# A hand-ordered attention and feed-forward kernel: GpSimd's queue, its loads, the sketches and the task list rearranged

## The chip, the cores and the metric

The kernel runs on one core of a Trainium2 chip. The metric is device time in microseconds for one execution, lower is better. Several executions were timed, and one execution was recorded by the hardware profiler; the profile's times count from the start of its span.

## The reference

Polynomial-sketch attention, then a feed-forward layer with SiLU. There are 4 batches, 4 heads, a sequence of 1088 and a head size of 32; the sketches S1 and S2 are 8 by 32. The feed-forward part has 4352 tokens of width 128 and an inner width of 2048.

```python
def phi(x):
    a = np.einsum('rd,bhsd->bhsr', S1, x)
    b = np.einsum('rd,bhsd->bhsr', S2, x)
    return np.einsum('bhsi,bhsj->bhsij', a, b).reshape(*x.shape[:-1], r * r)
q_p, k_p = phi(q), phi(k)
kv = np.einsum('bhsf,bhsd->bhfd', k_p, v)
z = np.sum(k_p, axis=2)
num = np.einsum('bhsf,bhfd->bhsd', q_p, kv)
den = np.einsum('bhsf,bhf->bhs', q_p, z)[..., None] + 1e-06
attn = num / den                                   # [B, H, S, D]
x = attn.transpose(0, 2, 1, 3).reshape(B * S, H * D)
h = x @ w_in
out = (h * (1.0 / (1.0 + np.exp(-h)))) @ w_out     # float32 [4352, 128]
```

## The kernel before

The order of all work is written out by hand. `ORDER` is a list of tasks, read from top to bottom; each task emits its instructions, and every engine executes what it was given in that order. An engine stops at an instruction whose inputs are not there, and all that stands behind it on that engine waits too. Loads are emitted ahead of the whole list: on SyncE's queue (SP) K of batch 0 in two pieces, the first part of Q, V, the four quarters of w_in, the rest of Q, then K and Q of batches 1 to 3; on ScalarE's queue the two sketches; on GpSimd's queue w_out and V of batches 1 to 3, which these loads convert from float32 to bf16. GpSimd's queue first has its memsets and masks, then these loads, and after them whatever tasks give it.

Some loads are held. `begin(..., after)` adds a dependency on another load's landing: w_out waits for the second quarter of w_in, V of batch b waits for Q of batch b−1, K of batch b for the same, and Q of batch b for K of batch b.

The tasks, with the engine that does most of them; the first number is the batch, and a pair p0 p1 is a range of rows of 64 tokens:

- `weights` (DVE) transposes the sketches into ST and masks them into WK, the weights of pk and of the constant columns of WQ; `weights2` (DVE) makes the mask hm4 and L4 (S2 repeated for four heads and masked); `wq_const` (GpSimd) copies WK into the constant columns of WQ for all four batches, eight small copies.
- `kt` (DVE) transposes K; `pk` (PE) multiplies by WK; `tk` (DVE) transposes the result back to SBUF; `kp` (DVE) forms the products of features, four pieces a batch.
- `zs` (PE) sums for z, `zc` copies it out of PSUM (A is ScalarE, V is VectorE), `mm` (PE) multiplies by L4, and `mk` (DVE) writes the last columns of WQ. `kv` (PE) accumulates kv; `kw` (DVE) or `kw_act` (ScalarE) copies it out with masks.
- `qt` (DVE) transposes Q; `pq` (PE) multiplies by WQ; `tq` (DVE) transposes back; `dn` (DVE, four instructions) forms and applies the denominator; `qo` (DVE) forms the feature products; `pt` (DVE) transposes them; `nm` (PE) multiplies by kv; `xc` copies the result to xT, the tokens of the feed-forward part.
- `wic` (ScalarE) converts a quarter of w_in to bf16, `vc0` half of V of batch 0.
- `f1 c s` (PE), `sl c s` (ScalarE, SiLU) and `f2 c s` (PE) are the feed-forward part for chunk c of tokens and slice s of the inner width; `ot` (DVE) transposes the output of a chunk and stores it through SP's queue. There are ten chunks; the first three have 256, 384 and 448 tokens.
- `zeros n` (PE) are n matmuls of zeros, 128 by 128 by 128, whose result nobody reads.

A tile named with H takes one of the two PSUM buffers of f1. The pool of f1 has two buffers, those of f2's output, of pk, pq and nm (psP), and of z, m and kv (psA) one each.

Of the kernel before, what the change touches and what calls it, by code (L numbers as in the profile page):

```python
# [28 lines left out]
f2 0 1, f2 0 2, qo 0 10 17, f1 1 0, sl 1 0, f1 1 4
zs 1, f1 1 2, sl 1 4, f2 0 3, f1 1 1, zc 1 A  # L30
pk 2, sl 1 2, ot 0, pt 0 10 17, sl 1 1, f1 1 6
qt 1 0 34, f2 1 0, f1 1 3, tk 2, mm 1, f2 1 1
sl 1 6, f1 1 5, f2 1 2, mk 1, kp 1 0 1, nm 0 10 17
sl 1 3, pq 1 0 8 H, kp 1 1 1, sl 1 5, xc 0 10 17 A, tq 1 0 8
kp 1 0 0, f1 1 7, kp 1 1 0, f2 1 3, pq 1 8 17, f1 2 0
dn 1 0 8, f2 1 4, sl 1 7, f1 2 4, sl 2 0, kv 1
f1 2 1, sl 2 4, f2 1 5, f1 2 7, sl 2 1, f2 1 6
f2 1 7, kw 1, qo 1 0 8, f1 2 6, sl 2 7, ot 1
pt 1 0 8, zs 2, f1 2 3, sl 2 6, zc 2 V, tq 1 8 17
f2 2 0, f1 2 2, sl 2 3, dn 1 8 17, mm 2, nm 1 0 8  # L40
xc 1 0 8 V, f1 2 5, mk 2, f2 2 1, sl 2 2, kt 3 0 34
sl 2 5, qt 2 0 34, f2 2 2, f2 2 3, f1 3 1, qo 1 8 17
f2 2 4, f1 3 0, f2 2 5, sl 3 1, f2 2 6, f1 3 6
f2 2 7, sl 3 0, ot 2, pt 1 8 17, sl 3 6, f1 3 2
pq 2 0 8, f1 3 5, f2 3 0, sl 3 2, tq 2 0 8, f1 3 3
sl 3 5, kp 2 0 0, f2 3 1, nm 1 8 17, f1 3 7, sl 3 3
f2 3 2, sl 3 7, xc 1 8 17 V, f1 3 4, pk 3, dn 2 0 8
kp 2 1 1, f1 4 1, f2 3 3, sl 3 4, f1 4 3, kp 2 1 0
kp 2 0 1, f2 3 4, sl 4 1, sl 4 3, f2 3 5, f1 4 4
f2 3 6, f1 4 0, kv 2, qo 2 0 8, sl 4 4, tk 3  # L50
pt 2 0 8, kw 2, f1 4 2, f2 3 7, sl 4 0, pq 2 8 17 H
sl 4 2, ot 3, tq 2 8 17, nm 2 0 8, f1 4 6, f2 4 0
xc 2 0 8 V, f1 4 5, zs 3, sl 4 6, sl 4 5, f1 5 2
f2 4 1, zc 3 V, sl 5 2, f1 5 4, dn 2 8 17, qo 2 8 17
qt 3 0 34, f2 4 2, pt 2 8 17, f2 4 3, kp 3 0 1, f1 4 7
kp 3 1 0, mm 3, sl 5 4, f1 5 0, sl 4 7, f2 4 4
sl 5 0, f2 4 5, f1 5 3, f2 4 6, f1 5 1, mk 3
f2 4 7, sl 5 3, ot 4, sl 5 1, f1 5 6, nm 2 8 17
xc 2 8 17 V, sl 5 6, f1 5 5, f2 5 0, sl 5 5, f2 5 1
f1 5 7, f2 5 2, f1 6 0, pq 3 0 8, sl 5 7, kp 3 1 1  # L60
f1 6 3, f2 5 3, f2 5 4, sl 6 0, f1 6 2, sl 6 3
f2 5 5, tq 3 0 8, kp 3 0 0, sl 6 2, dn 3 0 8, f1 6 4
qo 3 0 8, f2 5 6, f1 6 1, pt 3 0 8, kv 3, sl 6 4
f1 6 6, sl 6 1, f2 5 7, sl 6 6, kw 3, ot 5
f1 6 7, pq 3 8 17, nm 3 0 8 H, sl 6 7, f2 6 0, f1 6 5
f2 6 1, xc 3 0 8 V, sl 6 5, f1 7 3, sl 7 3, f2 6 2
f2 6 3, f1 7 2, tq 3 8 17, f2 6 4, f1 7 0, dn 3 8 17
sl 7 2, sl 7 0, qo 3 8 17, pt 3 8 17, f2 6 5, f2 6 6
f1 7 1, f2 6 7, ot 6, f1 7 4, sl 7 1, sl 7 4
nm 3 8 17, f1 7 7, f2 7 0, sl 7 7, f1 7 5, sl 7 5  # L70
xc 3 8 17 V, f2 7 1, f1 8 0, sl 8 0, f2 7 2, f1 7 6
f2 7 3, f1 8 1, f2 7 4, sl 7 6, f1 8 2, sl 8 1
f2 7 5, f1 8 7, f2 7 6, f2 7 7, sl 8 2, f1 8 3
sl 8 7, ot 7, sl 8 3, f1 8 4, f2 8 0, sl 8 4
f2 8 1, f1 8 5, f2 8 2, sl 8 5, f1 8 6, f2 8 3
f2 8 4, f1 9 0, sl 8 6, f2 8 5, f1 9 1, sl 9 0
f2 8 6, f2 8 7, sl 9 1, f1 9 2, f1 9 3, sl 9 2
# [12 lines left out]
def kernel(  # L90
# [65 lines left out]
    def begin(eng, dst, src, after=None):  # L156
        ins = eng.dma_start(dst, src)  # L157
# [10 lines left out]
    def load_v(eng, b, dst, after=None):  # L168
        for c in range(4):
            n = min(NC, NY - c * NC)  # L170
            ins = begin(eng, dst[32 * c: 32 * (c + 1), :, :n, :].rearrange("p h n d -> p h (n d)"),
                        AP(tensor=v.tensor, offset=v[b, 0, c * NC].offset,
                           ap=[[NY * D, 32], [S * D, H], [1, n * D]]), after)
        return ins

    def sketch(eng, i, src):
        return eng.dma_start(T12[:, i, :], AP(tensor=src.tensor, offset=src.offset,
                                              ap=[[0, P // R], [D, R], [1, D]]))
# [12 lines left out]

# [22 lines left out]
    prev = q0b
    for b in range(1, B):
        load_v(nc.gpsimd, b, Vb[b], prev)
        kb = load_kq(nc.sync, b, k, Kx, after=prev)
        prev = load_kq(nc.sync, b, q, Qx, after=kb)  # L220

    nc.scalar.activation(out=warm, in_=warm, func=ACT.Silu)


# [11 lines left out]
            nc.tensor.matmul(t["zps"][:, :ncol], zw, zw[:, :ncol], start=True, stop=True)  # L236

    def weights():
        vcopy_in = T12.rearrange("p a d -> p (a d)")
        nc.vector.transpose(out=ST.rearrange("p a c i -> p (a c i)"), in_=vcopy_in)  # L240
        nc.vector.tensor_tensor(out=WK, in0=ST[:, :, 0:2, :].rearrange("p a h i -> p h a i"),
                                in1=bcast(bcast(hm2, 2, 2), 3, R), op=ALU.mult)

    def weights2():
        nc.vector.tensor_reduce(out=hm4, in_=E8.rearrange("p s h -> p h s"), axis=AX.X, op=ALU.add)  # L245
        nc.vector.tensor_tensor(out=L4, in0=bcast(T12[:, 1, :], 1, H), in1=bcast(hm4, 2, D),
                                op=ALU.mult)

    def wq_const():
        for b in range(B):  # L250
            nc.gpsimd.tensor_copy(out=WQ[b][:, :, 0:R].rearrange("p h (i e) -> p h e i", e=2),
                                  in_=WK[:, :, 0, :].rearrange("p h (e i) -> p h e i", e=2))
            nc.gpsimd.tensor_copy(out=WQ[b][:, :, R: 2 * R], in_=WK[:, :, 1, :])  # L253

# [21 lines left out]
        nc.vector.transpose(out=t["pk", b].rearrange("p n r h a i -> p r n (h a i)"),  # L278
                            in_=t["pk_ps", b][:, :, :NC * 32].rearrange("p r (n f) -> p r n f", f=32))

    def kp(b, e, h):
        s = t["pk", b][:, :, :, h].rearrange("p n r a i -> p (n r) a i")
        o = t["kp", b][:, :, :, e, h].rearrange("p n r j i -> p (n r) j i")
        nc.vector.tensor_tensor(out=o, in0=bcast(s[:, :, 0, 4 * e: 4 * e + 4], 2, R),  # L284
                                in1=bcast(s[:, :, 1], 3, 4), op=ALU.mult)
# [86 lines left out]

    def qo(b, p0, p1):
        fa, fb, fw = feats(b, p0, p1)
        if p0 == 0:
# [2 lines left out]
        nc.vector.tensor_tensor(out=t["qp", b][:, p0:p1].rearrange("p y r j i -> p (y r) j i"),  # L378
                                in0=bcast(fa, 2, R), in1=bcast(fb, 3, R), op=ALU.mult)
# [127 lines left out]
```

## Time and profile before

| what | value |
|---|---|
| median of 3 runs | 122.09 us (121.97 to 122.43) |
| profiled execution | 121.77 us, its span 119.1 us |
| busy in the span | PE 88.3, ACT 73.3, DVE 67.6, GpSimd 12.1 us |
| mean granted TensorE clock | 0.912 |
| moved by DMA | 8.81 MB read from HBM, 2.23 MB written |

Busy time is the sum of the spans of an engine's instructions; instructions that issue a DMA are not counted as busy on the queues of SP and ScalarE. Lines L157, L230 and L227 are those of helpers (all loads, and the copies on ScalarE and VectorE), so there one goes by the tile. In the waits, a line names the engine that stood still, the one that released it, and the total time, the number of times, and the longest. The chain is followed back from the last instruction to what released each step.

### The profile page before, as it was taken

The numbers are of one execution on the slowest core, as the hardware profiler recorded it, in microseconds if no ns is written. First come the engines' busy times: TensorE is split into PE (matmuls) and PEld (weight loads), VectorE is DVE, ScalarE is ACT, GpSimd is POOL, SyncE is SP. The second block draws the span as 40 slices with busy tenths as digits, with TensorE's granted clock in tenths as the row PEclk, the third lists the DMA queues.
The fourth block names the chain that finished last, engine by engine and source line by source line (L and its number), as shares of the span: only waits on it lengthen the run. The fifth ranks groups of instructions, "written<-read, shape, count | busy, mean of one in ns | idle before, by whom it ended". The sixth has DMA issues, their size and how long they took to land.

```text
span 119.1 us, 2189 instructions
## 1 busy us (share of the span) xinstructions
PE 88.3 (74%) x857; PEld 48.1 (40%) x864; DVE 67.6 (57%) x128; ACT 73.3 (62%) x91; POOL 12.1 (10%) x47
## 2 busy tenths in 40 slices
...
GB/s 99 288 265 279 125 277 122 151 243 195 148 192 129 6 0 0 44 6 3 66 6 19 61 0 0 90 3 0 88 0 6 47 41 70 18 1 67 21 102 22
DMA packets 24857, 9.81 MB, mean 82 GB/s; under 512 B 21392, under 2 KB 23184, under 8 KB 24848
## 3 DMA queue, kind: packets, MB, share of 16 engines
...
q10 hardware_dynamic: 288, 0.03, 0.2%
q14 instruction: 3, 0.02, 0.1%
HBM read 8.81 MB, written 2.23 MB: 93 GB/s over the span
## 4 chain that ended last, share of the span: by engine, by line
PE 42%; DMA 23%; DVE 17%; ACT 8%; issue 2%; SPq 2%; POOL 2%; POOLq 0%; ACTq 0%; DVEq 0%
PE o_ps L437 18%; PE h_ps L419 16%; DMA Qx<-in_q_dram 11%; DMA Kx<-in_k_dram 9%; ACT g L426 8%; DVE qp L378 3%; DMA T<-in_S_dram 3%; DVE kp L284 2%; DVE PQ L358 2%; PE zps L236 2%; DVE KT L258 2%; SPq L157 2%; POOL Vb L157 2%; PE pq_ps L352 2%; DVE qT L384 1%
## 5 line engine op out<-in xcount | busy, mean ns | idle before, releaser
L426 ACT ACTIVATE g<-h_ps 128x1024 bf16<-128x1024 f32 (+2 forms) x72 | 65.5, 981 | 7.8 <-PE h_ps L419 5.7
L419 PE MATMUL h_ps<-xT,w_in_bf 128*128 128x512 bf16 (+4 forms) x156 | 39.8, 347 | 0.5
L437 PE MATMUL o_ps<-g,w_out_bf 128*128 128x512 bf16 (+4 forms) x157 | 37.5, 346 | 0.4
L437 PEld LDWEIGHTS <-w_out_bf 128*128 128x128 bf16 x160 | 15.2, 98 | 14.5 <-issue 0.7
L419 PEld LDWEIGHTS <-w_in_bf 128*128 128x128 bf16 x160 | 14.2, 98 | 15.2 <-issue 5.6
L352 PE MATMUL pq_ps<-QT,WQ 64*64 64x288 f32 (+3 forms) x48 | 4.0, 409 | 21.6 <-POOL WQ L253 21.6
L358 DVE STREAM_TRANSPOSE PQ<-pq_ps 128x576 f32<-128x576 f32 (+3 forms) x6 | 4.0, 669 | 23.0 <-PE pq_ps L352 23.0
L335 ACT ACTIVATE KVw<-kv_ps,hm 64x64 bf16<-64x64 f32 (+1 forms) x6 | 1.5, 306 | 22.8 <-PE kv_ps L316 22.7
L443 DVE STREAM_TRANSPOSE o_tt<-o_ps 128x512 f32<-128x512 f32 (+4 forms) x10 | 6.3, 635 | 13.9 <-PE o_ps L437 13.8
L236 PE MATMUL zps<-zw 128*128 128x128 bf16 x112 | 10.7, 264 | 1.1 <-POOL hm L196 1.1
L284 DVE TENSOR_TENSOR kp<-pk 128x576 bf16<-128x576 f32 x16 | 11.3, 740 | 0.0
L352 PEld LDWEIGHTS pq_ps<-QT,WQ 64*64 64x64 f32 x48 | 1.4, 143 | 23.4 <-POOL WQ L253 21.7
L236 PEld LDWEIGHTS <-zw 128*128 128x128 bf16 x112 | 9.0, 123 | 3.7 <-issue 2.5
L378 DVE TENSOR_TENSOR qp<-PQ 128x1024 bf16<-128x1024 f32 (+4 forms) x9 | 10.3, 1146 | 0.1
L157 POOL DMA_DIRECT2D Vb<-in_v_dram x12 | 6.5, 546 | 15.2 <-DMA Qx<-in_q_dram 15.2
L384 DVE STREAM_TRANSPOSE qT<-qp 128x512 f32<-128x512 f32 (+4 forms) x9 | 5.9, 659 | 0.1
L258 DVE STREAM_TRANSPOSE KT<-Kx 128x1088 f32<-128x1088 f32 (+2 forms) x5 | 5.3, 1063 | 0.0
L341 DVE STREAM_TRANSPOSE QT<-Qx 128x1088 f32<-128x1088 f32 (+2 forms) x5 | 5.3, 1057 | 0.0
L230 ACT ACTIVATE Vb<-Vx 128x576 bf16<-128x576 f32 x2 | 1.3, 675 | 5.0 <-DMA Vx<-in_v_dram 5.0
L227 DVE CAST xT<-num_ps 128x576 bf16<-128x576 f32 (+1 forms) x5 | 3.6, 714 | 0.2
L271 PE MATMUL h_ps<-KT,WK 64*32 64x288 f32 x16 | 2.4, 682 | 1.8 <-DVE hm L245 1.8
L316 PEld LDWEIGHTS <-kp 128*128 128x128 bf16 x72 | 3.1, 107 | 0.7 <-DVE kp L284 0.2
...
## 6 DMA issues: line engine op xcount, KB each, us to landing
Kx<-in_k_dram SPq DMA_DIRECT2D x3, 544.0 KB, 3.6
Qx<-in_q_dram SPq DMA_DIRECT2D x3, 544.0 KB, 4.1
...
Vb<-in_v_dram POOLq DMA_DIRECT2D x9, 72.0 KB, 3.8
w_out_bf<-in_moe_w_out_dram POOLq DMA_DIRECT2D x1, 512.0 KB, 7.0
...
```

Source lines behind the costliest of these rows:

```text
L157: ins = eng.dma_start(dst, src)
L236: nc.tensor.matmul(t["zps"][:, :ncol], zw, zw[:, :ncol], start=True, stop=True)
L258: nc.vector.transpose(out=KT[b % 2][:, y0 * 32: y1 * 32], in_=Kx[b][:, y0:y1, :].rearrange("p a d -> p (a d)"))
L284: nc.vector.tensor_tensor(out=o, in0=bcast(s[:, :, 0, 4 * e: 4 * e + 4], 2, R), in1=bcast(s[:, :, 1], 3, 4), op=ALU.mult)
L352: nc.tensor.matmul(t["pq_ps", b, p0][64 * g: 64 * (g + 1), r, :cols].rearrange("p (y x) -> p y x", x=32), w[rs, :], qv[rs, g, p0:p1, :], s ...
L358: nc.vector.transpose(out=PQ[b % 2][:, p0:p1].rearrange("p y r f -> p r y f"), in_=t["pq_ps", b, p0][:, :, :cols].rearrange("p r (y f) -> ...
L378: nc.vector.tensor_tensor(out=t["qp", b][:, p0:p1].rearrange("p y r j i -> p (y r) j i"), in0=bcast(fa, 2, R), in1=bcast(fb, 3, R), op=ALU ...
L384: nc.vector.transpose(out=dst.rearrange("p r (y x) -> p y r x", x=32), in_=src)
L419: nc.tensor.matmul(h[:, i, :], w_in_bf[:, j * P: (j + 1) * P], xT[:, t0: t0 + ntok], start=True, stop=True)
L426: nc.scalar.activation(out=gv, in_=t.pop(("h", c, s)), func=ACT.Silu)
L437: nc.tensor.matmul(op[c][:, :ntok], w_out_bf[:, j, :], g[:, i, :], start=(j == 0), stop=(j == NJ - 1))
L443: nc.vector.transpose(out=o_tt[:, :ntok], in_=op[c][:, :ntok])
```

## The change

GpSimd's copies of constants (`wq_const`) stay a task, and the GpSimd loads become tasks too: `wo` (w_out) and `lv b` (V of batch b) now come behind `wq_const` in the list. None of the loads is held, except w_out, which waits for V of batch 0. K and Q of batches 1 to 3 are issued by SP in one go after the others.

w_out is read in groups of four rows: partition p of group i holds rows 512 i + 4 p to 512 i + 4 p + 3. So that f1 makes the inner columns in the same arrangement, `wic` reads every fourth column of its quarter of w_in.

The sketches are loaded to 32 partitions, S1 twice and S2 twice, and four transposes spread them over the 128 partitions; a third load puts S2 on all partitions, for L4, whose product moves from VectorE to GpSimd.

The task list is new throughout; its start is shown. The counts of zero matmuls are different at each place.

```diff
 ORDER = """
-weights, kt 0 0 18, zeros 28, pk 0 0 2 H, weights2, kt 0 18 34
-vc0 2 4, qt 0 0 8, vc0 0 2, zeros 6, pk 0 2 4, tk 0
-kp 0 1 1, zeros 13, zs 0, kp 0 0 0, zc 0 A, kp 0 0 1
-wic 1, wq_const, wic 0, zeros 10, mm 0, mk 0
-wic 2, zeros 6, pq 0 0 4, kp 0 1 0, zeros 4, kv 0
-tq 0 0 4, dn 0 0 4, wic 3, qt 0 8 34, zeros 22, pq 0 4 10 H
-qo 0 0 4, pt 0 0 4, pq 0 10 17, kw_act 0, zeros 3, nm 0 0 4 H
-xc 0 0 4 A, tq 0 4 10, zeros 10, f1 0 0, sl 0 0, f1 0 1
-kt 1 0 34, dn 0 4 10, zeros 10, f1 0 3, sl 0 1, sl 0 3
-tq 0 10 17, f2 0 0, qo 0 4 10, f1 0 2, pt 0 4 10, sl 0 2
-pk 1, dn 0 10 17, nm 0 4 10 H, tk 1, xc 0 4 10 A, kt 2 0 34
+weights, vc0 0 2, kt 0 0 18, kt 0 18 34, zeros 33, pk 0 0 2 H
+weights2, zeros 3, pk 0 2 4, qt 0 0 8, tk 0, zeros 13
+zs 0, vc0 2 4, kp 0 0 0, wic 1, wic 0, zc 0 V
+wq_const, kp 0 0 1, zeros 5, mm 0, kp 0 1 0, mk 0
+zeros 14, pq 0 0 4 H, kp 0 1 1, tq 0 0 4, zeros 7, kv 0
+dn 0 0 4, kw_act 0, qo 0 0 4, wic 3, pt 0 0 4, wic 2
+zeros 27, nm 0 0 4 H, qt 0 8 34, xc 0 0 4 V, zeros 7, pq 0 4 10
+f1 0 0, tq 0 4 10, sl 0 0, f1 0 1, wo, sl 0 1
+pq 0 10 17, dn 0 4 10, qo 0 4 10, tq 0 10 17, zeros 3, f1 0 2
+f2 0 0, f1 0 3, sl 0 2, f2 0 1, pt 0 4 10, kt 1 0 34
+sl 0 3, nm 0 4 10 H, f2 0 2, xc 0 4 10 A, f2 0 3, dn 0 10 17
+f1 1 0, sl 1 0, ot 0, f1 1 3, sl 1 3, pk 1
+qo 0 10 17, f1 1 1, tk 1, f1 1 6, kt 2 0 34, f2 1 0
+sl 1 1, qt 1 0 34, lv 1, lv 2, f1 1 7, f2 1 1
...
-    T12 = const.tile([P, 2, D], FP32, name="T12")
-    ST = const.tile([P, 2, 4, R], FP32, name="ST")
+    T16 = const.tile([32, D], FP32, name="T16")
+    T2 = const.tile([P, D], FP32, name="T2")
+    ST = const.tile([P, 2, 2, R], FP32, name="ST")
...
-    def sketch(eng, i, src):
-        return eng.dma_start(T12[:, i, :], AP(tensor=src.tensor, offset=src.offset,
-                                              ap=[[0, P // R], [D, R], [1, D]]))
+    def sketch(eng, dst, src, count):
+        return eng.dma_start(dst, AP(tensor=src.tensor, offset=src.offset,
+                                     ap=[[0, count], [D, R], [1, D]]))
...
-    sketch(nc.scalar, 0, S1)
-    sketch(nc.scalar, 1, S2)
+    sketch(nc.scalar, T16[0:16, :], S1, 2)
+    sketch(nc.scalar, T16[16:32, :], S2, 2)
     load_kq(nc.sync, 0, k, Kx, 18, NY)
     load_kq(nc.sync, 0, q, Qx, 0, 8)
-    load_v(nc.sync, 0, Vx)
-    wi = []
+    sketch(nc.scalar, T2, S2, P // R)
+    v0 = load_v(nc.sync, 0, Vx)
     for i in range(4):
-        wi.append(begin(nc.sync, w_in_f[:, i * CH:(i + 1) * CH], moe_w_in[:, i * CH:(i + 1) * CH]))
-    q0b = load_kq(nc.sync, 0, q, Qx, 8, NY)
+        begin(nc.sync, w_in_f[:, i * CH:(i + 1) * CH], moe_w_in[:, i * CH:(i + 1) * CH])
+    load_kq(nc.sync, 0, q, Qx, 8, NY)
+    for b in range(1, B):
+        load_kq(nc.sync, b, k, Kx)
+        load_kq(nc.sync, b, q, Qx)
...
-    wo = begin(nc.gpsimd, w_out_bf, moe_w_out.rearrange("(j p) m -> p j m", p=P), wi[1])
-    prev = q0b
-    for b in range(1, B):
-        load_v(nc.gpsimd, b, Vb[b], prev)
-        kb = load_kq(nc.sync, b, k, Kx, after=prev)
-        prev = load_kq(nc.sync, b, q, Qx, after=kb)
-
...
     def weights():
-        vcopy_in = T12.rearrange("p a d -> p (a d)")
-        nc.vector.transpose(out=ST.rearrange("p a c i -> p (a c i)"), in_=vcopy_in)
-        nc.vector.tensor_tensor(out=WK, in0=ST[:, :, 0:2, :].rearrange("p a h i -> p h a i"),
+        for i in range(4):
+            nc.vector.transpose(out=ST[32 * i: 32 * (i + 1)].rearrange("p a h i -> p (a h i)"), in_=T16)
+        nc.vector.tensor_tensor(out=WK, in0=ST.rearrange("p a h i -> p h a i"),
                                 in1=bcast(bcast(hm2, 2, 2), 3, R), op=ALU.mult)
 
     def weights2():
         nc.vector.tensor_reduce(out=hm4, in_=E8.rearrange("p s h -> p h s"), axis=AX.X, op=ALU.add)
-        nc.vector.tensor_tensor(out=L4, in0=bcast(T12[:, 1, :], 1, H), in1=bcast(hm4, 2, D),
-                                op=ALU.mult)
+        nc.gpsimd.tensor_tensor(out=L4, in0=bcast(T2, 1, H), in1=bcast(hm4, 2, D), op=ALU.mult)
...
+    def wo():
+        begin(nc.gpsimd, w_out_bf.rearrange("p (i e) m -> p i (e m)", e=4),
+              moe_w_out.rearrange("(i p e) m -> p i (e m)", p=P, e=4), v0)
+
+    def lv(b):
+        load_v(nc.gpsimd, b, Vb[b])
...
-    def wic(i, n=4):
-        w = DFF // n
-        acopy(w_in_bf[:, i * w: (i + 1) * w], w_in_f[:, i * w: (i + 1) * w])
+    def wic(i):
+        cols = slice(i * CH, (i + 1) * CH)
+        acopy(w_in_bf[:, cols].rearrange("p (e m) -> p e m", e=4),
+              w_in_f[:, cols].rearrange("p (m e) -> p e m", e=4))
```

Further down the new list, `lv 3` and the rest of the tasks follow in an order of their own; xc 1 0 8 and zc 2 are on ScalarE there instead of VectorE. That `qo` makes its tiles where they aren't there yet, and that `kp` can take another engine, changes no instruction.

More of the change, by code (lines that the diff above doesn't have):

```diff
@@ L27 @@
-tq 0 10 17, f2 0 0, qo 0 4 10, f1 0 2, pt 0 4 10, sl 0 2
-pk 1, dn 0 10 17, nm 0 4 10 H, tk 1, xc 0 4 10 A, kt 2 0 34
[L29 to L77, printed above, removed]
@@ L78 @@
-ot 8, f2 9 0, f2 9 1, sl 9 3, f2 9 2, f2 9 3
-ot 9
+weights, vc0 0 2, kt 0 0 18, kt 0 18 34, zeros 33, pk 0 0 2 H
[7 more added lines that the diff above has]
+pq 0 10 17, dn 0 4 10, qo 0 4 10, tq 0 10 17, zeros 3, f1 0 2
@@ new lines @@
+f2 0 0, f1 0 3, sl 0 2, f2 0 1, pt 0 4 10, kt 1 0 34
[3 more added lines that the diff above has]
+sl 1 1, qt 1 0 34, lv 1, lv 2, f1 1 7, f2 1 1
+sl 1 6, pt 0 10 17, f1 1 2, sl 1 7, sl 1 2, zs 1
+pk 2, f1 1 5, zc 1 A, mm 1, tk 2, f1 1 4
+sl 1 5, sl 1 4, f2 1 2, f2 1 3, nm 0 10 17 H, xc 0 10 17 A
+mk 1, zs 2, kp 1 1 0, pq 1 0 8, kp 1 0 0, f1 2 3
+f1 2 1, kp 1 0 1, f2 1 4, zc 2 A, f2 1 5, f2 1 6
@@ new lines @@
+sl 2 3, sl 2 1, f1 2 0, f2 1 7, sl 2 0, f1 2 5
+tq 1 0 8, kp 1 1 1, sl 2 5, kv 1, f1 2 2, sl 2 2
+dn 1 0 8, ot 1, f2 2 0, f1 2 4, sl 2 4, qo 1 0 8
+kw 1, f2 2 1, f1 2 6, sl 2 6, f2 2 2, pt 1 0 8
+kt 3 0 34, pq 1 8 17, nm 1 0 8 H, f1 2 7, f2 2 3, xc 1 0 8 A
+sl 2 7, f2 2 4, f1 3 0, sl 3 0, tq 1 8 17, pk 3
+f1 3 1, f2 2 5, lv 3, sl 3 1, dn 1 8 17, qo 1 8 17
+pt 1 8 17, f1 3 5, mm 2, f2 2 6, tk 3, f1 3 7
+mk 2, sl 3 5, sl 3 7, f2 2 7, f1 3 2, ot 2
+nm 1 8 17, f1 3 3, f2 3 0, sl 3 2, f2 3 1, qt 2 0 34
@@ new lines @@
+sl 3 3, xc 1 8 17 V, f1 3 6, kp 2 1 1, f2 3 2, sl 3 6
+f1 4 2, kp 2 0 0, pq 2 0 8, f1 4 3, tq 2 0 8, kp 2 1 0
+sl 4 2, f2 3 3, sl 4 3, f1 3 4, pq 2 8 17, kp 2 0 1
+sl 3 4, f1 4 7, sl 4 7, dn 2 0 8, kv 2, tq 2 8 17
+f1 4 1, sl 4 1, f2 3 4, qo 2 0 8, kw 2, f1 4 0
+f2 3 5, sl 4 0, f2 3 6, pt 2 0 8, f2 3 7, ot 3
+f1 4 6, f1 4 4, nm 2 0 8, zs 3, f2 4 0, sl 4 6
+sl 4 4, xc 2 0 8 V, dn 2 8 17, qt 3 0 34, f1 4 5, f2 4 1
+f1 5 1, f2 4 2, qo 2 8 17, sl 4 5, zc 3 V, sl 5 1
+f2 4 3, f1 5 0, sl 5 0, f2 4 4, kp 3 1 1, f1 5 5
@@ new lines @@
+f2 4 5, f2 4 6, f1 5 4, sl 5 5, sl 5 4, f2 4 7
+pt 2 8 17, f1 5 7, mm 3, nm 2 8 17, kp 3 1 0, f1 5 3
+sl 5 7, ot 4, mk 3, f2 5 0, f1 5 2, xc 2 8 17 V
+sl 5 3, sl 5 2, pq 3 0 8, f1 5 6, sl 5 6, f2 5 1
+tq 3 0 8, f1 6 1, sl 6 1, pq 3 8 17, f1 6 4, kp 3 0 0
+f2 5 2, dn 3 0 8, sl 6 4, f1 6 2, f2 5 3, tq 3 8 17
+qo 3 0 8, kp 3 0 1, f2 5 4, f1 6 0, sl 6 2, f2 5 5
+f1 6 7, pt 3 0 8, kv 3, dn 3 8 17, sl 6 0, kw 3
+sl 6 7, f1 6 5, f2 5 6, f2 5 7, f1 6 6, sl 6 5
+nm 3 0 8, f1 6 3, ot 5, xc 3 0 8 V, sl 6 6, f2 6 0
```

24 lines of the change are left out of this document (18 added, 6 removed).

## The prediction

> **What bounds the kernel now.** I read the busy time by stages first, then the waits, then GpSimd's own timeline, then the chain that ended last. The stages (window, its length, then busy time of PE, PEld, DVE, ACT and POOL, granted clock, DMA share, GB/s):
>
> ```profile
> 0.00:12.20 12.20, 8.84 (x117) 6.25 (x117) 5.42 (x13) 4.37 (x8) 4.50 (x27) 1.00 0.75 228
> 12.20:33.30 21.10, 0.02 (x3) 0.02 (x3) 0.62 (x1) 0.62 (x2) 6.87 (x15) 0.60 0.85 185
> ...
> 39.20:58.00 18.80, 18.26 (x252) 10.94 (x250) 18.26 (x38) 16.18 (x22) 0.00 (x0) 1.00 0.06 12
> 58.00:87.70 29.70, 29.42 (x236) 13.14 (x241) 26.66 (x48) 26.40 (x28) 0.00 (x0) 1.00 0.19 32
> 87.70:113.90 26.20, 25.89 (x168) 12.89 (x168) 11.67 (x21) 23.78 (x26) 0.00 (x0) 1.00 0.20 35
> ```
>
> From 12.2 to 33.3 us nothing computes: PE 0.02, DVE 0.62, ACT 0.62 of 21.1 us. After 39.2 PE is busy 73.6 of 74.7 us, so that part can hardly shrink. The waits (engine, line, releaser; total, times, longest) say what ends the hole:
>
> ```profile
> DVE PQ L358 <- PE pq_ps L352: 23.0, 2, 21.2
> ...
> PE pq_ps L352 <- POOL WQ L253: 21.6, 1, 21.6
> POOL Vb L157 <- DMA Qx<-in_q_dram: 15.2, 3, 7.9
> ```
>
> The first pq matmul waits 21.6 us for WQ, eight small GpSimd copies. GpSimd's timeline (start, length) shows why they are late, and SyncE's pieces of the chain show what GpSimd's loads wait for:
>
> ```profile
> 9.91 1.29 POOL L157 DMA_DIRECT2D w_out_bf<-in_moe_w_out_dram  x1 [5.56 <-DMA w_in_f<-in_moe_w_in_dram]
> ...
> 30.71 2.15 POOL L157 DMA_DIRECT2D Vb<-in_v_dram  x4 [5.90 <-DMA Qx<-in_q_dram]
> 32.90 0.20 POOL L251 COPY WQ<-WK 128x16 f32<-128x16 f32 x1
> ```
> ```profile
> 6.20 6.08 DMA Qx<-in_q_dram
> ...
> 12.30 6.78 DMA Kx<-in_k_dram
> ```
>
> The copies stand behind the V loads on GpSimd, and each V load is held until the Q load of the batch before has landed. Their input WK has been there since 5.3 us.
>
> **The change part by part.** *(a) The constant copies go ahead of the loads.* To place the new start I follow the path to the first f1 with durations of these rows:
>
> ```profile
> 0.82 1.27 ACTq L177 DMA_DIRECT2D T<-in_S_dram  x2
> ...
> 1.08 3.17 PE L236 MATMUL zps<-zw 128*128 128x128 bf16 x28 [1.08 <-POOL hm L196]
> ...
> 4.75 0.25 DVE L240 STREAM_TRANSPOSE ST<-T 128x64 f32<-128x64 f32 x1 [4.75 <-DMA T<-in_S_dram]
> ...
> 5.21 0.77 DVE L258 STREAM_TRANSPOSE KT<-Kx 128x576 f32<-128x576 f32 x1
> ...
> 6.04 1.18 PE L271 MATMUL h_ps<-KT,WK 64*32 64x288 f32 x8 [1.79 <-DVE hm L245]
> ...
> 6.27 0.70 DVE L258 STREAM_TRANSPOSE KT<-Kx 128x512 f32<-128x512 f32 x1
> ...
> 8.61 1.26 ACT L230 ACTIVATE Vb<-Vx 128x576 bf16<-128x576 f32 x2 [4.99 <-DMA Vx<-in_v_dram]
> ...
> 9.15 0.78 DVE L278 STREAM_TRANSPOSE pk<-h_ps 128x576 f32<-128x576 f32 x1 [1.86 <-PE h_ps L271]
> ...
> 9.97 2.10 DVE L284 TENSOR_TENSOR kp<-pk 128x576 bf16<-128x576 f32 x3
> ...
> 10.65 2.17 ACT L230 ACTIVATE w_in_bf<-w_in_f 128x512 bf16<-128x512 f32 x4
> ...
> 11.98 0.17 DVE L306 TENSOR_TENSOR WQ<-m_ps,hm 128x16 f32<-128x16 f32 x1
> ```
>
> The eight copies end about 1.2 us after they start (32.90 to 34.06). In the new order GpSimd first does L4 (a 128x128 product, moved from DVE). Its bounds: 0.2 us, one of the copies, up to 1.6 us, if it cost eight times a copy of 16 columns. Both inputs are there by some 6.5 us (the reduce follows both KT transposes; T2 is a third issue behind the two that took 1.27). So WQ's constants are ready by 7.9 to 9.3 us; mk, the last writer of WQ, comes later, and the copies cost nothing. If they slipped past 11.4 us, every further us would count in full.
>
> *(b) Sketches in 32 rows.* The two issues end at 2.1 (0.82 + 1.27) and the second lands 2.65 us later, at 4.75. The small T16 pair lands between 3.4 (half of that way) and 4.75 us (as now); I take 4.2. Four small transposes replace one of 0.25: between 0.25 and 1.0 us together, I take 0.6, between the ends because a fixed part is repeated. With 0.2 for WK, KT starts at 5.0 instead of 5.21 (bounds 3.9 to 6.0): worth little. The reduce and L4 no longer stand between the KT halves, which end at 6.4 instead of 6.97.
>
> *(c) Zero matmuls.* In the old list 28+6+13+10+6+4+22+3+10+10 = 112, in the new one 33+3+13+5+14+7+27+7+3 = 112, and still 128 columns each: only their places change. The first 28 took 0.113 us each, so 33 end at 4.8, before pk is ready at 5.8. The two pk halves (1.18 each, three zeros between) end at 8.4 at the old pace, or at 6.9 if the longer run has brought the matmuls up to the pace of later ones; I take 8.1, nearer the old pace, since a gap of 1 us follows as before. tk starts at 8.1 instead of 9.15.
>
> *(d) The new order from there*, on DVE: tk 0.78 to 8.9; three kp of 0.70, the z copy and mk of 0.17 each: mk ends at 11.35. So pq 0 0 4 starts at about 11.4 instead of 33.28. The next rows give the rest:
>
> ```profile
> 33.28 0.70 PE L352 MATMUL pq_ps<-QT,WQ 64*64 64x128 f32 x8 [21.57 <-POOL WQ L253]
> ...
> 34.05 0.45 DVE L358 STREAM_TRANSPOSE PQ<-pq_ps 128x256 f32<-128x256 f32 x1 [21.24 <-PE pq_ps L352]
> ...
> 34.32 1.17 PE L316 MATMUL kv_ps<-Vb,kp 128*128 128x64 bf16 x18
> ...
> 35.51 1.04 DVE L341 STREAM_TRANSPOSE QT<-Qx 128x832 f32<-128x832 f32 x1
> 35.53 1.59 ACT L335 ACTIVATE KVw<-kv_ps,hm 128x64 bf16<-128x64 f32 x6 [22.70 <-PE kv_ps L316]
> 36.47 0.65 DVE L378 TENSOR_TENSOR qp<-PQ 128x512 bf16<-128x512 f32 x1
> 37.16 0.45 DVE L384 STREAM_TRANSPOSE qT<-qp 128x256 f32<-128x256 f32 x1
> ...
> 38.43 0.31 PE L393 MATMUL h_ps<-qT,KVw 64*64 64x128 bf16 x8
> ...
> 38.79 0.39 ACT L230 ACTIVATE xT<-h_ps 128x256 bf16<-128x256 f32 x1 [1.67 <-PE h_ps L393]
> ...
> 39.23 1.04 PE L419 MATMUL h_ps<-xT,w_in_bf 128*128 128x256 bf16 x8
> ```
>
> DVE: kp 0.70 to 12.05, tq 0.45, dn 1.0 (34.50 to 35.51), qo 0.65, pt 0.45: 14.6. PE and ACT: seven zeros and kv, then kw_act 1.59, end at about 15.0; nm ends at 15.4. DVE does qt 0 8 34 (1.04) first, 15.65, then xc 0 0 4, which moves from ACT to DVE: 16.1. This qt needs the second Q0 load, landed at 12.28 now; w_out, now released by V0 (8.61) and not by w_in (9.91), runs beside it. It may land up to 3 us later with w_out wholly ahead of it; 14.6 is when it is wanted. I add 0.3. **First f1 at 16.4 instead of 39.23.**
>
> *(e) The rest.* From the first f1 to the end it is 79.9 us now (119.1 − 39.2), with PE busy for all but 1.1 us of it up to 113.9. The tasks are the same. tq 0 4 10 and most of a kt move behind the first f1, and tq 1 8 17 and dn 1 8 17 move behind xc 1 0 8: DVE's work up to xc 1 0 8 stays within 0.4 us, set off by seven fewer zeros after the first f1. So 79.9 again.
>
> *(f) Loads without holds, w_out in groups of four rows.* What is late next is data. The sizes (KB each, median us to landing) and the rates:
>
> ```profile
> Kx<-in_k_dram SPq DMA_DIRECT2D x3, 544.0 KB, 3.6
> ...
> Vb<-in_v_dram POOLq DMA_DIRECT2D x9, 72.0 KB, 3.8
> w_out_bf<-in_moe_w_out_dram POOLq DMA_DIRECT2D x1, 512.0 KB, 7.0
> ```
> ```profile
> 9.00:12.00 3.00, 2.71 (x71) 2.38 (x67) 2.81 (x5) 2.29 (x6) 1.29 (x1) 1.00 0.72 272
> 12.00:15.00 3.00, 0.00 (x0) 0.00 (x0) 0.82 (x3) 0.82 (x2) 2.16 (x4) 1.00 1.33 130
> 15.00:18.00 3.00, 0.00 (x0) 0.00 (x0) 0.00 (x0) 0.00 (x0) 0.00 (x0) 0.70 1.33 281
> ```
>
> DVE wants K1 at about 20 us (after xc: tq, dn, qo, tq, pt), K2 some 4.5 us later, at 24.3 (kt 1, dn, qo, tk). After Q0 at 12.3 three loads of 544 KB are in front of K2's end, and at worst all of w_out and V (512 + 12 x 72 KB): 3.08 MB. At 272 GB/s K2 lands at 23.6, no stall. At 130 GB/s for GpSimd's 1.41 MB (the window when w_out in its old form ran almost alone) it is 5.6 us later, a stall of 4.9. The window with K1 and V1 together shows 281, and w_out's pieces become longer, so I stay near the first end: 0.3 us. In groups of four rows wic reads every fourth column; no row shows such a read. Bounds: the 0.62 a copy of the contiguous form, or twice that. wic 3 and wic 2 follow kw_act at 15.0 and end at 16.1, the first Silu comes at 17.0, so up to 0.9 us more is hidden.
>
> A rule beside that last row: the Trainium skill, Advanced Engine Details and Errata, section Memory Cachelines, says SBUF wants at least two hits on a 16-byte line for full speed, and this read makes one. No run here shows such a read yet. If each copy doubled, the first Silu would come 0.2 us later and the sum would be 99.8.
>
> **Sum:** 16.4 + 79.9 + 0.3 = 96.6 us of span. The profiled execution took 121.77 for a span of 119.1, 2.67 around it: 99.3. The median of the runs (122.09) is 0.3 above the profiled one: **99.6 us**, faster by 22.5.
>
> **The rivals.**
> *Loads in each other's way* (0.20). Without holds V2 and V3 run beside K1, Q1, K2 though they are wanted much later. For it: K1 took 6.78 us beside w_out and V1, where a K load's median is 3.6. If each of K1, Q1, K2 took 6.8 from 12.3 on, K2 would land at 32.6 were they in series; at 130 GB/s for GpSimd's bytes at 29.2. DVE then waits 4.9 us at kt 2, PE runs out of work of the first two chunks, and the time is 102 to 106, centre 104.
> The Trainium skill, DMA: Bandwidth & Descriptors, section Queues, rings and completion order, says each DMA engine goes round its queues packet by packet; K1's 6.78 agrees, and by that rule this rival holds while GpSimd's queue is full.
> *A quicker start* (0.08): T16 at 3.4, pk at the later pace, f1 at 14.5 and PE's 1.1 idle us gone: 96 or less.
> *The change doesn't do what it says* (0.04): the copies run early, but another wait, on L4, T2 or V0, holds POOL or PE; a landing of 7 us as for w_out would cost 7 to 15 us of the gain: 107 to 115.
> *Slower* (0.03): the hole goes, but the granted clock stays low. In the hole it was 0.60 on average; with other gaps between the zeros it could fail to rise. PE's 73.6 us at clock c take 73.6/c; the gain of 22.5 is gone when c is below 73.6/96.1 = 0.77. At 0.6 the end would be 49 us later, 149. Against it: 1.00 in all windows once PE is fed.
>
> **How the numbers follow.** Forecast 0.65, rivals 0.20, 0.08, 0.04, 0.03. The forecast's own range is 97.0 to 101.5 (f1 between 15 and 18). With most of the load rival: 96.0 to 104.0. Half a per cent, 0.6 us, is about what can be told from no change. Faster 0.95, same 0.02, slower 0.03: only the clock rival, and the tail of the last but one, are not faster.
>
> **What would show it.** (a) GpSimd's copies before 10 us, PE's wait for them gone from the waits. (b) DVE's first transpose at 4.2 or sooner; four of them under 0.25 each. (c) the pk groups 1.18 or shorter. (d) pq at 11.4, first f1 at 16.4. (e) PE busy over 98% from there to 5.2 us before the end. (f) no idle DVE in front of kt 1, kt 2, qt 1 with a K or Q load as releaser; ACT's wic copies 0.62. It is wrong if PE or DVE idles between 16 and 35 us for a load, if Q0's second part lands after 15, or if the granted clock after 15 us is under 1.00.

## The result and the profile after

The changed kernel took 104.77 us (103.92 to 105.12, four runs) against 122.03 for the kernel before: a ratio of 0.858, interval 0.851 to 0.865. It is faster by 17 us where 22.5 were forecast, and it lies outside the range of 96 to 104. The profiled execution took 105.12 us with a span of 103.1. Single executions of some kernels ran over 1.5% above the fastest of the same kernel; the times and ratios here and below leave them out.

The stages, with the same columns as those of before:

```profile
0.00:12.20 12.20, 8.09 (x107) 5.63 (x107) 4.56 (x13) 4.89 (x6) 7.21 (x40) 0.86 0.75 218
12.20:18.30 6.10, 5.39 (x100) 4.46 (x101) 5.55 (x13) 3.17 (x8) 2.15 (x5) 1.00 1.06 354
18.30:23.20 4.90, 2.28 (x27) 1.36 (x23) 4.63 (x9) 3.36 (x4) 0.00 (x0) 1.00 1.10 338
23.20:28.00 4.80, 4.77 (x32) 2.93 (x32) 1.90 (x7) 1.68 (x3) 1.81 (x4) 0.64 1.05 165
28.00:58.00 30.00, 29.78 (x332) 14.13 (x330) 28.88 (x51) 26.70 (x34) 0.90 (x2) 1.00 0.18 27
58.00:97.90 39.90, 39.24 (x282) 18.59 (x274) 22.20 (x41) 35.96 (x39) 0.00 (x0) 1.00 0.22 38
```

The hole of 21 us is gone. A small one has come: from 18.3 to 23.2 us PE is busy for 2.28 of 4.9 us, and in the 4.8 us after it the granted clock is 0.64 and DVE and ACT are busy for 1.90 and 1.68 us only. The waits name it, and the issues give the landing (KB, us):

```profile
POOL Vb L158 <- DMA w_out_bf<-in_moe_w_out_dram: 9.1, 1, 9.1
...
PE o_ps L439 <- DMA w_out_bf<-in_moe_w_out_dram: 2.6, 1, 2.6
```
```profile
Kx<-in_k_dram SPq DMA_DIRECT2D x3, 544.0 KB, 10.4
Qx<-in_q_dram SPq DMA_DIRECT2D x3, 544.0 KB, 14.8
...
w_out_bf<-in_moe_w_out_dram POOLq DMA_DIRECT2D x1, 512.0 KB, 13.5
```

In the timeline the load goes out at 9.64 and the first f2 starts 13.6 us later:

```profile
8.20 0.40 POOL L242 TENSOR_TENSOR L<-T,hm 128x128 f32<-128x128 f32 x1 [3.84 <-DVE hm L241]
...
9.64 0.94 POOL L158 DMA_DIRECT2D w_out_bf<-in_moe_w_out_dram  x1
...
13.54 0.45 PE L354 MATMUL h_ps<-QT,WQ 64*64 64x128 f32 x8 [0.26 <-DVE WQ L308]
...
16.66 2.14 ACT L226 ACTIVATE w_in_bf<-w_in_f 128x512 bf16<-128x512 f32 x2
...
18.26 1.05 PE L421 MATMUL h_ps<-xT,w_in_bf 128*128 128x256 bf16 x8
...
23.23 0.61 PE L439 MATMUL o_ps<-g,w_out_bf 128*128 128x256 bf16 x4 [2.65 <-DMA w_out_bf<-in_moe_w_out_dram]
```

pq starts at 13.54 and waits no longer for GpSimd's copies; the first f1 starts at 18.26. From there to the end it is 84.8 us, where the kernel before took 79.9.

### The profile page after: what moved, and what is told of

Read it like the earlier page. It is cut to its first block, busy times and chain, and to the rows that moved or that the text cites. A ratio compares the mean times of both kernels' runs of the same rounds, so it can differ in the third digit from the quotient of the medians.

```text
span 103.1 us, 2192 instructions
## 1 busy us (share of the span) xinstructions
PE 89.6 (87%) x864; PEld 47.1 (46%) x864; DVE 67.7 (66%) x130; ACT 75.8 (73%) x91; POOL 12.1 (12%) x48
## 4 chain that ended last, share of the span: by engine, by line
PE 63%; DMA 16%; DVE 9%; ACT 1%; POOL 1%; ACTq 1%; issue 1%; DVEq 0%; POOLq 0%
PE o_ps L439 28%; PE h_ps L421 25%; DMA w_out_bf<-in_moe_w_out_dram 13%; DMA T<-in_S_dram 3%; PE pq_ps L354 3%; PE num_ps L395 2%; ACT g L428 1%; DVE PQ L360 1%; DVE kp L286 1%; PE z_ps L295 1%; PE pk_ps L273 1%; DVE KT L260 1%; ACTq L178 1%; DVE o_tt L445 1%; DVE qp L380 1%; PE kv_ps L318 1%
## 5 line engine op out<-in xcount | busy, mean ns | idle before, releaser
L439 PE MATMUL o_ps<-g,w_out_bf 128*128 128x512 bf16 (+4 forms) x160 | 38.7, 355 | 2.8 <-DMA w_out_bf<-in_moe_w_out_dram 2.6
L421 PE MATMUL h_ps<-xT,w_in_bf 128*128 128x512 bf16 (+4 forms) x160 | 40.8, 351 | 0.1
L232 PE MATMUL zps<-zw 128*128 128x128 bf16 x112 | 9.6, 249 | 1.1 <-POOL hm L199 1.1
L232 PEld LDWEIGHTS <-zw 128*128 128x128 bf16 x112 | 8.1, 115 | 3.5 <-issue 2.3
L360 DVE STREAM_TRANSPOSE PQ<-pq_ps 128x512 f32<-128x512 f32 (+3 forms) x8 | 5.7, 714 | 1.7 <-PE pq_ps L354 1.6
L354 PE MATMUL pq_ps<-QT,WQ 64*64 64x256 f32 (+3 forms) x64 | 5.3, 401 | 0.1
L236 DVE STREAM_TRANSPOSE ST<-T 32x32 f32<-32x32 f32 x4 | 0.8, 202 | 5.6 <-DMA T<-in_S_dram 5.6
L226 ACT ACTIVATE w_in_bf<-w_in_f 128x512 bf16<-128x512 f32 x4 | 4.3, 1122 | 0.1
## 6 DMA issues: line engine op xcount, KB each, us to landing
w_out_bf<-in_moe_w_out_dram POOLq DMA_DIRECT2D x1, 512.0 KB, 13.5
```

Source lines behind the costliest of these rows:

```text
L354: nc.tensor.matmul(t["pq_ps", b, p0][64 * g: 64 * (g + 1), r, :cols].rearrange("p (y x) -> p y x", x=32), w[rs, :], qv[rs, g, p0:p1, :], s ...
L360: nc.vector.transpose(out=PQ[b % 2][:, p0:p1].rearrange("p y r f -> p r y f"), in_=t["pq_ps", b, p0][:, :, :cols].rearrange("p r (y f) -> ...
L421: nc.tensor.matmul(h[:, i, :], w_in_bf[:, j * P: (j + 1) * P], xT[:, t0: t0 + ntok], start=True, stop=True)
L439: nc.tensor.matmul(op[c][:, :ntok], w_out_bf[:, j, :], g[:, i, :], start=(j == 0), stop=(j == NJ - 1))
```

## The experiments

**Why does w_out land 13.5 us after its issue, when it took 7.0 before?** The theory: with the holds gone, six K and Q loads of 544 KB stand in SP's queue, and w_out shares the DMA engines with them. Three kernels tell it from its rivals.

K and Q of batches 1 to 3 held until w_out has landed (`kq_held`):

```diff
     def wo():
-        begin(nc.gpsimd, w_out_bf..., moe_w_out..., v0)
+        wo_in = begin(nc.gpsimd, w_out_bf..., moe_w_out..., v0)
+        for b in range(1, B):          # and no longer ahead of the tasks
+            load_kq(nc.sync, b, k, Kx, after=wo_in if b == 1 else None)
+            load_kq(nc.sync, b, q, Qx)
```

> The changed kernel with K and Q of batches 1 to 3 issued only after w_out has landed; all else as changed. Theory (w_out's landing, 13.5 us after its issue, is late because it takes turns on the DMA engines with the six K and Q loads that stand in SP's queue): w_out lands 6 to 8 us after its issue, near 16.5 us, PE's wait of 2.65 us for it and the half clock behind it go, time 100 to 101.5. Rival one (V1 and V2, issued right behind w_out on its own queue, slow it): landing still 12 us or more, time 104 to 107. Rival two (the form with groups of four rows is slow by itself): the same as rival one. If K1 then comes too late (wanted at 22 us), DVE stalls in front of kt 1 and the time stays near 104 though w_out landed early.

Measured: 100.32 us, a ratio to before of 0.826 (0.818 to 0.835), span 98.4. w_out's issue and landing, and the stretch behind the first f1:

```profile
DMA to landing us min/median/max: 8.2/8.2/8.2
```
```profile
18.20:23.20 5.00, 4.74 (x55) 3.41 (x52) 4.70 (x10) 4.74 (x6) 2.55 (x5) 1.00 0.98 305
23.20:28.00 4.80, 4.60 (x87) 2.23 (x84) 4.70 (x10) 4.17 (x6) 0.00 (x0) 1.00 1.11 350
```

The landing is back at 8.2 us, though w_out still comes in groups of four rows and the V loads still stand behind it on its queue. PE is busy for 4.74 of 5.0 us where it was 2.28 of 4.9, and the clock stays at 1.00. The span is 4.7 us shorter. First f1 is at 18.19, as in the changed kernel, and the rest takes 80.2 us.

V of batches 1 to 3 held for w_out instead (`v_held`):

```diff
     def wo():
-        begin(nc.gpsimd, w_out_bf..., moe_w_out..., v0)
+        t['wo'] = begin(nc.gpsimd, w_out_bf..., moe_w_out..., v0)
     def lv(b):
-        load_v(nc.gpsimd, b, Vb[b])
+        load_v(nc.gpsimd, b, Vb[b], t['wo'])
```

> The changed kernel with V of batches 1 to 3 issued only after w_out has landed; K and Q free as changed. Theory (turns with SP's K and Q loads): w_out still lands 12 us or more after its issue, time 104 to 106. Rival one (its own queue's V loads): landing 6 to 9 us after the issue, time 100 to 102.

Measured: 105.27 us (ratio 0.865, 0.861 to 0.869). w_out lands 15.3 us after its issue, and PE waits 4.4 us:

```profile
PE o_ps L439 <- DMA w_out_bf<-in_moe_w_out_dram: 4.4, 1, 4.4
```

That is no earlier than in the changed kernel: the V loads behind w_out on its own queue aren't the cause.

w_out in single rows as before, w_in copied in plain order (`wo_rows`):

```diff
-        begin(nc.gpsimd, w_out_bf.rearrange("p (i e) m -> p i (e m)", e=4),
-              moe_w_out.rearrange("(i p e) m -> p i (e m)", p=P, e=4), v0)
+        begin(nc.gpsimd, w_out_bf, moe_w_out.rearrange("(j p) m -> p j m", p=P), v0)
-        acopy(w_in_bf[:, cols].rearrange("p (e m) -> p e m", e=4),
-              w_in_f[:, cols].rearrange("p (m e) -> p e m", e=4))
+        acopy(w_in_bf[:, cols], w_in_f[:, cols])
```

> The changed kernel with w_out read in single rows as before and w_in converted in its plain order (no strided read). Theory (turns with other queues): with four times as many and shorter pieces w_out gets a smaller share of each turn and lands later, 16 us or more after its issue, and the time is 106 to 110, though the four copies of w_in take 0.62 us again instead of 1.12. Rival two (the grouped form is slow): w_out lands 7 to 9 us after its issue as in the kernel before, time 100 to 102. Rival three (the strided read of w_in is what costs): time 1 to 2 us lower whatever w_out does.

Measured: 107.80 us (ratio 0.884, 0.879 to 0.889). Landing 16.5 us after the issue, PE's wait 5.7. So the single rows cost 2.5 to 3 us beside the unheld loads: the versions in groups of four rows took 104.6 to 105.3. How much of this is the landing isn't shown, since in `copies_no_holds`, below, single rows landed after 15.2 us, like the groups of four in `v_held`. The copies of w_in are short again:

```profile
16.05 1.15 ACT L226 ACTIVATE w_in_bf<-w_in_f 128x512 bf16<-128x512 f32 x2
```

Two take 1.15 us together where the strided ones take 2.14, and nothing is gained by it: first f1 at 17.65 is set by nm and qt, and PE waits for w_out after it.

**What does the low clock add to the wait?** 45 zeros are put where PE waits (`zeros_fill`):

```diff
-pq 0 10 17, dn 0 4 10, qo 0 4 10, tq 0 10 17, zeros 3, f1 0 2
+pq 0 10 17, dn 0 4 10, qo 0 4 10, tq 0 10 17, zeros 3, f1 0 2, zeros 45
 f2 0 0, ...
```

> The changed kernel with 45 more zero matmuls between the third f1 and the first f2, where PE waits 2.65 us for w_out. Theory (the late w_out costs twice: the wait, and the granted clock of 0.57 to 0.64 that follows it until 28 us): w_out lands as late as in the changed kernel, the granted clock from 23 to 28 us stays at 1.00, and the time is 1.5 to 2.2 us lower, 102.5 to 103.3. Rival (the low clock there falls on work that DVE and ACT bound anyway): clock 1.00 but time within 0.5 us of the changed kernel's.

Measured: 102.47 us (ratio 0.840, 0.834 to 0.847). The first f2 starts at 23.23, as in the changed kernel (w_out went out 0.9 us earlier and took 14.5 us to land), and the stretch after it is:

```profile
23.20:28.00 4.80, 4.57 (x51) 2.80 (x52) 1.97 (x3) 3.05 (x5) 2.31 (x5) 1.00 1.08 170
```

1.00 instead of 0.64, and from the first f2 to the end 77.1 us of span instead of 79.9. How much of these 2.8 us is the clock isn't shown: this run's first f1 came 2.1 us earlier (16.16 for 18.26), so DVE stood further ahead when f2 began. The time is 2.3 us lower, where 1.5 to 2.2 were forecast. Against the kernel with the hold, the late load costs 2.9 us until the first f2 (23.23 instead of 20.35) and 1.8 us after it (79.9 instead of 78.1).

**What does the first part of the change bring alone?** The kernel before, with the GpSimd loads and the later K and Q loads emitted behind the copies (`copies_alone`):

```diff
-wic 1, wq_const, wic 0, zeros 10, mm 0, mk 0
+wic 1, wq_const, loads, wic 0, zeros 10, mm 0, mk 0
...
-    wo = begin(nc.gpsimd, ...)      # ahead of all tasks
-    ...
+    def loads():                    # the same lines, now a task
+        wo = begin(nc.gpsimd, ...)
+        ...
```

> The kernel before with one edit: w_out, the V loads of batches 1 to 3 and the K and Q loads of batches 1 to 3 are emitted right behind the eight constant copies instead of ahead of all tasks; all holds, the old task list, the old sketches and the old w_out form stay. Theory (the place of the copies in GpSimd's queue made the hole): pq at about 12.2 us instead of 33.3, first f1 near 17.5 to 18; K1 (landing near 19 with the holds) then makes DVE wait 1 to 2 us at kt 1, and K2 (near 26) about 1 us; time 101.5 to 104. Rival (the loads without holds are what brings the gain, since held loads arrive only until 38 us): time 106 or more, with DVE standing at kt 2 and qt 1 for the held loads.

Measured: 103.79 us, ratio 0.851 (0.844 to 0.857). That is no less than the whole change gives (0.858, 0.851 to 0.865). First f1 is at 18.29, w_out lands 7.0 us after its issue, and DVE pays for the holds:

```profile
POOL Vb L157 <- DMA Qx<-in_q_dram: 15.7, 3, 8.2
...
DVE KT L259 <- DMA Kx<-in_k_dram: 2.8, 2, 1.7
```

GpSimd still waits 15.7 us for the Q loads, as before the change. Nothing stands behind it now, so it costs nothing.

The same, and V, K and Q of batches 1 to 3 without holds (`copies_no_holds`):

```diff
         for b in range(1, B):
-            load_v(nc.gpsimd, b, Vb[b], prev)
-            kb = load_kq(nc.sync, b, k, Kx, after=prev)
-            prev = load_kq(nc.sync, b, q, Qx, after=kb)
+            load_v(nc.gpsimd, b, Vb[b])
+            load_kq(nc.sync, b, k, Kx)
+            load_kq(nc.sync, b, q, Qx)
```

> The kernel before with the copies ahead of the loads (as in copies_alone, 103.79) and, in addition, V, K and Q of batches 1 to 3 without holds; w_out keeps its hold and its single rows. Theory (without holds w_out takes turns with six K and Q loads): w_out lands 15 us or more after its issue at 10.4, so near 26, PE waits 4 to 6 us in front of the first f2 with the clock falling after it, and the time is 106 to 109, 3 to 5 us more than with the holds, though DVE's waits of 2.8 us for K1 and K2 go. Rival (holds cost more than they bring): 101 to 103.

Measured: 105.70 us (ratio 0.872, 0.863 to 0.882): about 2 us slower than with the holds, less than the 3 to 5 expected. PE's wait is at the low end of what was expected:

```profile
PE o_ps L437 <- DMA w_out_bf<-in_moe_w_out_dram: 4.0, 1, 4.0
```
```profile
21.00:24.00 3.00, 0.00 (x0) 0.00 (x0) 1.90 (x6) 0.75 (x1) 0.00 (x0) 0.74 1.64 194
24.00:27.00 3.00, 2.48 (x24) 1.26 (x24) 0.00 (x0) 0.56 (x1) 2.24 (x5) 0.50 1.05 130
```

w_out lands 15.2 us after its issue, PE does nothing from 21 to 24 us, and the clock falls to 0.50; DVE's waits for K1 and K2 are gone. So here too the holds on what isn't urgent were protecting w_out.

The changed kernel was run once more beside these (`after_again`).

> The changed kernel once more, beside the two above on the same chip. From its first timing: 103.9 to 105.1, w_out landing 13 to 15 us after its issue, PE's wait for it 2 to 3 us, a granted clock below 0.8 from 24 to 27 us.

Measured: 104.48 and 105.30 us (ratio 0.867, 0.854 to 0.879). Its profile, of an execution of 106.94 us, shows w_out landing 15.4 us after the issue and PE waiting 4.6, above what was expected from the first profile. In all profiles with groups of four rows and six loads in SP's queue the landing lies between 13.5 and 15.4 us, so a single one tells it to about 2 us.

**Why was the start late too?** The sketches on 128 partitions as before, L4 on GpSimd (`sketch_128`):

```diff
-    sketch(nc.scalar, T16[0:16, :], S1, 2)
-    sketch(nc.scalar, T16[16:32, :], S2, 2)
-    sketch(nc.scalar, T2, S2, P // R)
+    sketch(nc.scalar, T12[:, 0, :], S1, P // R)
+    sketch(nc.scalar, T12[:, 1, :], S2, P // R)
-        for i in range(4):
-            nc.vector.transpose(out=ST[32 * i: 32 * (i + 1)]..., in_=T16)
+        nc.vector.transpose(out=ST..., in_=T12...)
```

> The changed kernel with the sketches loaded to 128 partitions as before (two loads, one transpose), L4 still on GpSimd from that tile. Theory (the two loads to 16 partitions land later, 5.6 instead of 4.75 us, and four transposes cost 0.6 us more than one): first pk at 6.0 to 6.2 instead of 7.47, first f1 about 1.4 us earlier, w_out's issue about 0.9 us earlier (then set by V of batch 0), time 1 to 1.4 us lower, 103.4 to 103.8. Rival (the start doesn't matter, since w_out's landing sets when f2 can begin): time within 0.5 us of the changed kernel's.

Measured: 104.61 us (ratio 0.859, 0.855 to 0.862), the same as the changed kernel: the rival. pk starts 1.07 us earlier (6.40 for 7.47), but f1 only 0.3 us (17.94 for 18.26). PE's rows of the two kernels show where the rest went, the changed one first:

```profile
7.47 1.18 PE L273 MATMUL h_ps<-KT,WK 64*32 64x288 f32 x8 [3.03 <-DVE KT L260]
...
10.14 1.18 PE L232 MATMUL zps<-zw 128*128 128x128 bf16 x13
```
```profile
6.40 1.18 PE L270 MATMUL h_ps<-KT,WK 64*32 64x288 f32 x8 [1.63 <-DVE KT L257]
...
9.07 1.57 PE L230 MATMUL zps<-zw 128*128 128x128 bf16 x13
...
10.57 0.72 PE L292 MATMUL z_ps<-pk 128*32 128x16 f32 x36
```

The 13 zeros in front of zs take 1.57 us instead of 1.18, and zs itself 0.72 instead of 0.50: PE was still slow then, and zs stood behind the zeros.

With the hold added (`held_sketch`, the two edits above together):

> The changed kernel with K and Q of batches 1 to 3 held for w_out and with the sketches on 128 partitions as before. Theory (with w_out out of the way the start counts): first f1 0.3 us earlier, as with the sketches alone (17.9 instead of 18.3), time 99.8 to 100.2 against 100.3 with the hold alone. Rival (the earlier pk is worth its full 1.1 us): 99.0 to 99.4.

Measured: 100.09 us (ratio 0.821, 0.814 to 0.828) against 100.32 with the hold alone, within what can be told; first f1 at 17.84.

And with 50 zeros in front of pk instead of 33 (`held_sketch_50`):

```diff
-weights, vc0 0 2, kt 0 0 18, kt 0 18 34, zeros 33, pk 0 0 2 H
+weights, vc0 0 2, kt 0 0 18, kt 0 18 34, zeros 50, pk 0 0 2 H
```

> As the kernel with the hold and the old sketches, but 50 zero matmuls instead of 33 in front of the first pk, so that PE is busy from 1.1 us until pk's inputs are there (about 6.3 us). Theory (the early matmuls run at half pace because PE stood idle from 4.4 us until pk): the pk groups take about 0.4 to 0.6 us instead of 1.18, tk starts 1.5 us earlier, and the zeros of 13 in front of zs take 0.75 instead of 1.57: first f1 1.5 to 2 us earlier, time 98 to 98.8. Rival (the pace doesn't come from the idle time): 50 zeros at 0.113 us end at 6.7, pk stays at 1.18, time within 0.5 us of the one with 33.

The early matmuls got faster, as the theory says, though not as much:

```profile
1.08 4.51 PE L227 MATMUL zps<-zw 128*128 128x128 bf16 x50 [1.08 <-POOL hm L194]
...
6.29 0.69 PE L270 MATMUL h_ps<-KT,WK 64*32 64x288 f32 x8 [0.69 <-DVE KT L257]
...
15.88 1.05 PE L418 MATMUL h_ps<-xT,w_in_bf 128*128 128x256 bf16 x8
```

pk takes 0.69 instead of 1.18, and f1 starts at 15.88, 2 us earlier. That the longer row of zeros did this isn't shown. In the profile of `zeros_fill`, whose start is that of the changed kernel with 33 zeros, pk was as quick, though PE had stood idle for 1.79 us before it, longer than the 1.65 of `held_sketch`:

```profile
1.08 3.70 PE L232 MATMUL zps<-zw 128*128 128x128 bf16 x33 [1.08 <-POOL hm L199]
...
6.56 0.69 PE L273 MATMUL h_ps<-KT,WK 64*32 64x288 f32 x8 [1.79 <-DVE KT L260]
...
16.16 1.05 PE L421 MATMUL h_ps<-xT,w_in_bf 128*128 128x256 bf16 x8
```

Of the eight profiles with 33 zeros one had the quick pk, and so had the two with 50. What sets the early pace stays open.

The time is 99.03 us (98.95 to 100.16, three runs; ratio 0.811, 0.802 to 0.821), just above the theory's range. The profile is of the run at 100.16, and in it the gain was given back to a new wait:

```profile
DVE KT L257 <- DMA Kx<-in_k_dram: 2.2, 1, 2.2
```

K1 had been held until w_out landed at 16.2 us, and is now wanted at 19.7.

So K1 goes out unheld, and the rest behind w_out, K2 ahead of Q1 (`k1_free`):

```diff
-        for b in range(1, B):
-            load_kq(nc.sync, b, k, Kx, after=wo_in if b == 1 else None)
-            load_kq(nc.sync, b, q, Qx)
+        load_kq(nc.sync, 1, k, Kx)
+        load_kq(nc.sync, 2, k, Kx, after=wo_in)
+        load_kq(nc.sync, 1, q, Qx)
+        load_kq(nc.sync, 2, q, Qx)
+        ...                            # K3, Q3
```

> The kernel with the hold, the old sketches and 50 zeros, but K of batch 1 goes out unheld ahead of w_out, and behind w_out's landing the order is K2, Q1, Q2, K3, Q3. Theory (in the one with 50 zeros the 2 us gained at the start were given back to a 2.2 us wait of DVE for K1, held until w_out landed at 16.2): K1 lands by 18.5, w_out by 18.5 too, kt 1 starts at 19.7 without a wait, first f1 stays at 15.9, and the time is 97.8 to 98.6. Rival (K1 takes its turns from w_out, which then lands at 19 or later): PE waits for w_out about 1 us, time 98.8 to 100.

Measured: 98.62 us (98.35 to 99.16, six runs), ratio 0.815 (0.810 to 0.820): the upper end of the theory's range. The wait for K1 is gone: behind the first f1, PE waits for no load and DVE 0.2 us for Q1, though w_out lands 9.0 us after its issue. It is some 6 us below the changed kernel, run beside it; from the version before it (99.03 us, ratio 0.811) its time can't be told apart. PE is busy nearly throughout behind the first f1, at 16.45 in this run:

```profile
16.40:20.40 4.00, 3.74 (x43) 2.59 (x39) 3.64 (x9) 3.90 (x5) 2.11 (x4) 1.00 0.92 181
20.40:28.00 7.60, 7.40 (x110) 3.96 (x110) 7.32 (x12) 6.14 (x11) 0.58 (x2) 1.00 1.03 296
28.00:92.00 64.00, 62.76 (x505) 29.74 (x512) 46.08 (x85) 57.71 (x64) 0.00 (x0) 1.00 0.21 39
```

## Why the prediction missed

**(a) The hole: right.** The copies end at 9.7 us, the wait of 21.6 us is gone, and `copies_alone` shows that their place in GpSimd's queue is worth all of the 17 us. L4 took 0.40 us on GpSimd, near the low bound.

**(b) to (d) The start: the place right, the size off.** First f1 came at 18.26 instead of 16.4. The term that was mis-sized most is (b): T16 landed at 5.59, not 4.2, and the four transposes took 0.85, not 0.6, so that the first pk started at 7.47 instead of 5.8. The small form buys no landing: over these runs the sketches, in either form, were there between 4.7 and 6.2 us. (c) had the pace of a pk group (1.18), but from the first pk to tk it was 2.8 us where the sum took 2.3. From tk to f1 the sum was 0.3 us too long. The start is not the same in every profile: in `zeros_fill`, with the changed kernel's start, the sketches landed at 4.68, pk took 0.69 and the first f1 came at 16.16, close to the 16.4 of the sum.

**(e) The rest: right.** With w_out out of the way it is 80.2 us (`kq_held`), as forecast with its 0.3 for loads.

**(f) The loads: this step failed.** It asked when K1 and K2 would be wanted, and these were in time: DVE never waits for them in the changed kernel, and DMA moved 338 to 354 GB/s from 12.2 to 23.2 us where the sum took 272. It did not ask the same of w_out, which went out on GpSimd's queue against the six loads in SP's. w_out is wanted by the first f2 at 20.6 us; at its old 7 us it would have landed at 16.6, and it landed at 23.2. That is 4.7 us of span (103.1 against 98.4 with the hold). The window of 130 GB/s, read in the sum as w_out almost alone, already had K1 (issued at 12.30) and V1 (from 12.59) in flight beside it. The rival of loads in each other's way (0.20) had the price, 102 to 106 with its centre at 104, but the wrong pair: it had GpSimd's V loads make K2 late, and the runs show SP's K and Q loads making w_out late, the V loads having no part in it (`v_held`). That its price fits is luck. The start's 1.9 and w_out's 4.6 (84.8 from the first f1 to the end instead of 80.2) are the whole difference between the 96.6 us of span that were summed up and the 103.1 measured, the rest cancels.

The rule set beside that rival (the Trainium skill, DMA: Bandwidth & Descriptors, section Queues, rings and completion order) is that the engines go round their queues packet by packet. The runs agree so far: w_out landed after 7 to 9 us with little or one K load beside it, and after 13.5 to 16.5 with six loads in SP's queue. That it is a round by packets no run shows by itself: in single rows, four times as many and shorter pieces, w_out landed after 16.5 us in `wo_rows` and after 15.2 in `copies_no_holds`, the latter no later than in groups of four.

With the other rule (the Trainium skill, Advanced Engine Details and Errata, section Memory Cachelines: at least two hits on a 16-byte line are needed) the trace agrees too: wic's copies, one element of four, took 1.12 us instead of 0.62. It cost nothing, since the last of them ended at 18.80 and the first Silu came at 18.91.

The quicker start did not come in the changed kernel, and the clock's rival, as a state that lasts, did not either; it came as a short stretch behind the wait for w_out.
